# Two tiles to a burst in the first pair's attention, and raw x laid out tile by tile

## The chip, the cores and the metric

The kernel runs on one core of a Trainium2 chip. The metric is the device time of one execution in microseconds (us); lower is better. TensorE (PE) multiplies matrices and writes to PSUM, a memory of eight banks; VectorE (DVE) and ScalarE (ACT) read PSUM and do the elementwise work; GpSimd (POOL) does elementwise work in SBUF; SyncE (SP) issues the DMAs.

## The reference

Attention over chunks of 64 tokens, and a mixture of four experts on its output, whose every expert sees every token:

```
scores = scale * matmul(q_c, k_c.T)          # per head and chunk of 64 tokens, 8 heads of 64
attn   = softmax(scores)
out    = matmul(attn, v_c)                   # -> x, 4608 tokens x 512
p      = domain_probs / sum(domain_probs)
for e in range(4):
    h = max(x @ w1[e], 0)                    # 512 -> 1024
    y += p[:, e] * (h @ w2[e])               # 1024 -> 512
```

All data are fp32. The products of the experts are made of three matmuls each, from a high and a low part of both factors.

## The kernel before

The 4608 tokens are nine sub-blocks of 512 (four tiles of 128 tokens each). The first sub-block goes through the experts alone, in eight plain passes (expert by half of the hidden units, n = 0 to 7). The other eight are four pairs; each pair goes through eight later passes, in which seven products of half-size blocks take the place of eight. While one pair is in the experts, the attention of the next pair is worked in between, so that TensorE always has the experts' matmuls to go on with. The attention of pair 0 lies beside the first sub-block's plain passes 1 to 6, that of pair 1 beside the later passes of pair 0, and so on.

A plain pass has eight steps of TensorE: four hidden blocks (`plain_hidden`, 12 matmuls of 128x128 by 512 columns, then a relu on ScalarE and its low part on VectorE) and four output tiles (`Tile.whole`, 12 matmuls, added into `acc` on VectorE). `issue` calls `beside.go()` before each step; `go` runs the generator `attention` up to its next `yield`. What is put into `deferred` there is written out after the step's own instructions. Each engine runs its instructions in the order in which the program writes them.

One tile of attention is 16 score matmuls of 64x64 (32 rows in the trace), a softmax (maximum, subtraction, exponential, sums, reciprocal, scaling), a transpose within blocks on VectorE, a placing copy on ScalarE (`a_place`) and 16 value matmuls. In pair 0 a tile takes five steps: `a_less_max` and `a_exps`, then `a_weights` and `a_transpose`, then `a_place`, then two steps of room. After them `a_next` writes a *burst*: the values of this tile and the scores of the next, 32 matmuls. There are nine such bursts in pair 0: scores alone, seven of both kinds, values alone. Scores stand in one half of `psa` (two PSUM banks of their own) and the values, as well as the softmax sums, in the other half. The tile's q and k come into `qk_in`, its v into `v_in`.

Pairs 2 and 3 already work two tiles to a burst (`attend_two`, `two_next`): the scores of both tiles fill both halves of `psa`, the values go into the banks B1 and C1, the sums into B1, and q, k and v of the odd tile are loaded into parts of `xraw` that are not yet filled with x. Pair 1 works tile by tile, and keeps its x in memory (`x_kept`) until `x_back` loads it.

The other six PSUM banks (A0, A1, B0, B1, C0, C1) are handed out in turn by `bank()` when no name is given: in plain passes every hidden block and output tile takes the next one, so that a bank comes round after six. The last plain pass and the later passes name theirs.

`xraw` holds the 1024 tokens of a pair as `[P, NK, PAIR * SUB]`: for each partition four rows of 1024 tokens; a tile is 128 columns of each row. The class `Tokens` makes from it the sums and the high and low parts that the later passes multiply.

Of the kernel before, what the change touches and what calls it, by code (L numbers as in the profile page):

```python
# [15 lines left out]
P = 128  # L16
# [15 lines left out]
def chunk_attention_moe(ctx: ExitStack, tc: tile.TileContext, qk, v, v0, dp, w1, w2, out):  # L32
# [180 lines left out]
    def a_copy(t):  # L213
        pair, i = divmod(t - NT, PAIR * NT)
        if pair == 1:
            tile_x = scratch[0][:, :SUB].rearrange("p (j q) -> p j q", j=NK)
        else:
            tile_x = of_tiles(pair, i, 1)
        to = tile_x.rearrange("p j (c q) -> p c j q", c=2)
        av = blocks(1)  # L220
        nc.scalar.copy(out=to[:, :, 0::2], in_=av[:, :, 0::2])
        nc.scalar.copy(out=to[:, :, 1::2], in_=av[:, ::-1, 1::2])
        if pair == 1:
            nc.sync.dma_start(out=x_kept[:, :, i * P : (i + 1) * P], in_=tile_x)

    def of_tiles(pair, i, n):
        if pair not in xraw:
            xraw[pair] = xpool.tile([P, NK, PAIR * SUB], F32, name="xraw")  # L230
        return xraw[pair][:, :, i * P : (i + n) * P]

    def two_load(t, i):
        if i == 0:
            a_load(t)
            return
        pair = (t - NT) // (PAIR * NT)
        to = of_tiles(pair, 6, 2).rearrange("p (g x) (h s) -> p g x h s", x=2, h=HG)
        st[t] = {"x": to}
        for g in range(2):  # L240
            nc.sync.dma_start(out=to[:, g], in_=qk[t, g].rearrange("c d x h s -> (c d) x h s"))

    def two_load_v(t, i, odd):
        if i and not odd:
            pair, j = divmod(t - NT, PAIR * NT)
            st[t]["v"] = of_tiles(pair, 7 if j == 7 else 5, 1).rearrange("p j (h d) -> p j h d", h=2)
        elif not odd:
            st[t]["v"] = load.tile([P, NK, 2, C], F32, name="v_in")
        to = st[t]["v"].rearrange("p (g i) h d -> p g i h d", i=2)
        of = v[t - NT].rearrange("p (g i h) d -> p g i h d", g=2, i=2)  # L250
        if not odd:
            nc.sync.dma_start(out=to[:, :, 0], in_=of[:, :, 0])
            return
        for half in range(2):
            rows, other = slice(half * C, (half + 1) * C), slice((1 - half) * C, (2 - half) * C)
            nc.sync.dma_start(out=to[rows, :, 1], in_=of[other, :, 1])
# [5 lines left out]
            q, k = (s["x"][of_half(c), head // HG, x, head % HG] for x in range(2))  # L262
            nc.tensor.matmul(s["sc"][of_half(half), c, slot], lhsT=q, rhs=k, start=True, stop=True)  # L263

    def two_sums(t):
        z = bank("B1")[:, : 2 * HG].rearrange("p (c j) -> p c j", c=2)
        st[t]["r"] = inverse_sums(st[t]["sc"], z)

    def two_weights(t):
        two_sums(t)  # L270
        a_scale(t)
        a_transpose(t)

    def two_next(t, scores):

        av = None
        if t is not None:
            av = [bank(name).rearrange("p (i j k) -> p i j k", i=2, k=C) for name in ("B1", "C1")]
            for i in range(2):
                s = st.pop(t + i)  # L280
                for c, half, slot, head in quarters():
                    nc.tensor.matmul(  # L282
                        av[half][of_half(slot % 2), i, head // 2],
                        lhsT=s["v"][of_half(half), head // 2, head % 2],
                        rhs=s["pt"][of_half(half), c, slot], start=True, stop=True,
                    )
        if scores is not None:
            for i in range(2):
                two_scores(scores + i, i)
        if av:  # L290
            pair, j = divmod(t - NT, PAIR * NT)
            to = of_tiles(pair, j, 2).rearrange("p j (i c q) -> p i j c q", i=2, c=2)
# [4 lines left out]
    x_kept = dram.tile([P, NK, PAIR * SUB], F32, name="x_kept")  # L297

    def x_back():
        xraw[1] = xpool.tile([P, NK, PAIR * SUB], F32, name="xraw")  # L300
        for k in range(NK):
            nc.sync.dma_start(out=xraw[1][:, k], in_=x_kept[:, k])


    def less_max(a):
# [15 lines left out]
    def scale(e, a, r):  # L321
        nc.vector.tensor_tensor(out=e, in0=a, in1=r, op=ALU.mult)

    def attention(pair, close):

        first = (1 + pair * PAIR) * NT
        last = first + PAIR * NT  # L330
        a_load(first)
        yield
        a_next(None, first)
        for t in range(first, last):

            if close:
                steps = (a_less_max, a_exps), (a_weights, a_transpose), (None, a_place), (None, None)
            else:
                steps = (a_less_max, a_exps), (a_sums, a_scale), (a_transpose, None), (a_place, None)
            for now, then in steps:  # L340
# [8 lines left out]
    def a_next(t, after, loads=True):  # L349
# [8 lines left out]
        if loads and after is not None:  # L358
            a_load_v(after)
            a_load_after(after)  # L360

# [69 lines left out]
    def hi_part(src, t):  # L431
        nc.scalar.copy(out=t[0], in_=src)
# [218 lines left out]
    class Tokens:  # L651
# [4 lines left out]
        def __init__(self, pair):  # L656
            x = xraw.pop(pair)
            for k in range(2):
                for s in range(2):
                    rows, toks = slice(2 * k, 2 * k + 2), slice(s * SUB, (s + 1) * SUB)  # L660
                    setattr(self, f"b{k + 1}{s + 1}", x[:, rows, toks])

        def less(self, name, a, b, out, eng=None):
            (eng or nc.vector).tensor_tensor(
# [2 lines left out]
            setattr(self, name, out)  # L667

        def sum1(self):
            self.less("t1", "b12", "b11", load.tile([P, 2, SUB], F32, name="qk_in"))  # L670

        def sum2(self):
            self.less("t2", "b22", "t1", self.b22)

        def sum2_apart(self, eng):

            self.t2 = [att.tile([P, SUB], F32, name=name) for name in ("e", "pt")]
# [3 lines left out]
        def sum4_apart(self):  # L681

            for k, t in enumerate(self.t2):
                nc.vector.tensor_tensor(out=psa[:, k], in0=self.b21[:, k], in1=t, op=ALU.subtract)
            self.t4 = psa

        def split2(self):
            i = self.KEYS["t2"]
            x_alloc(i)
            for k, t in enumerate(self.t2):  # L690
                hi_part(t, [part[:, k] for part in xt[i]])

        def lo2(self, k):
            lo_part(nc.vector, self.t2[k], [part[:, k] for part in xt[self.KEYS["t2"]]])

        def sum3(self, eng=None):
            self.less("t3", "b22", "b12", self.b12, eng)
# [4 lines left out]
        def hi(self, name):  # L702
            i = self.KEYS[name]
            x_alloc(i)
            hi_part(getattr(self, name), xt[i])

        def lo(self, name, eng=None):
            lo_part(eng or nc.vector, getattr(self, name), xt[self.KEYS[name]])


    TERMS = ((0, 0), (0, 1), (1, 0))
# [568 lines left out]
    class Beside:  # L1280


        def __init__(self, pair, close):
            self.steps = attention(pair, close)

        def go(self):
            next(self.steps, None)
# [188 lines left out]
    def attend(at, pair, places, i):  # L1476
        t = (1 + pair * PAIR) * NT + i
        after = t + 1 if i + 1 < PAIR * NT else None
        if i == 0:
            add(at, 13, lambda: a_next(None, t, False))  # L1480
# [4 lines left out]
        add(at, places[2], lambda: a_next(t, after, False))  # L1485
        if after:
            add(at, places[2] + 1, lambda: a_softmax(after))
            loads(at, places[2], after)
# [261 lines left out]
        by_halves(steps["b"])  # L1750

    with tc.manual_schedule():
        beside = Beside(0, True)
# [53 lines left out]
```

## Time and profile before

| | |
|---|---|
| median of 3 runs | 1480.26 us (1477.7 to 1481.23) |
| the profiled execution | 1478.61 us, span 1476.7 us |
| TensorE busy | 1461.3 us, 99% of the span |
| VectorE, GpSimd, ScalarE busy | 1094.4, 976.5, 623.3 us |
| TensorE's granted clock | full in all 40 slices |
| share of TensorE in the chain that ended last | 93% |

The span is from the first to the last instruction of the profiled execution. Busy time counts a matmul until its modelled end, so it overlaps with the next one; whether TensorE loses time is therefore read from the starts of its matmuls and from its waits.

### The profile page before, as it was taken

The page shows a single profiled execution, that of the slowest core. Times are in us where ns is not written, and L with a number is a line of the kernel's source. Part 1 is how long each engine was busy: PE and PEld are TensorE (multiplying, and loading weights), DVE is VectorE, ACT ScalarE, POOL GpSimd, SP SyncE. Part 2 cuts the span into 40 slices and gives each one's busy share as a digit, 9 for nine tenths or more (in the row PEclk, how much of TensorE's full clock was granted, in tenths as well). Part 3 has the DMA queues.
Part 4 walks back from the last instruction along what each step waited for, and adds up shares of the span by engine and source line. Part 5 has one row for each costly group of instructions (what it writes and reads, how often), then busy time and mean ns, then how long its engine had stood idle before and what let it go on. Part 6 is the DMA issues. An engine that isn't in the chain of part 4 may idle for free.

```text
span 1476.7 us, 23341 instructions
## 1 busy us (share of the span) xinstructions
PE 1461.3 (99%) x8556; PEld 1199.8 (81%) x8556; DVE 1094.4 (74%) x1492; ACT 623.3 (42%) x1165; POOL 976.5 (66%) x728
## 2 busy tenths in 40 slices
PE   8999999999999999999999999999999999999998
PEld 7888887887878878888888888888888888888887
DVE  5566658899898886787767977777668866666665
ACT  4556635545454534434433434444334333233332
POOL 5778887888877884555557656555557655555555
PEclk9999999999999999999999999999999999999999
DMA  9798886878777789766565688676565695565655
GB/s 308 266 342 313 302 316 209 272 240 266 237 252 240 241 260 259 241 219 230 194 210 198 219 231 279 218 241 198 195 203 197 201 255 198 198 207 194 207 190 151
DMA packets 201250, 346.94 MB, mean 235 GB/s; under 512 B 70176, under 2 KB 114480, under 8 KB 200752
## 3 DMA queue, kind: packets, MB, share of 16 engines
q1 hardware_dynamic: 201136, 345.45, 71.6%
q8 instruction: 68, 1.11, 0.3%
q14 instruction: 46, 0.38, 0.1%
HBM read 274.01 MB, written 71.38 MB: 234 GB/s over the span
## 4 chain that ended last, share of the span: by engine, by line
PE 93%; DVE 3%; DMA 2%; POOL 1%; issue 1%; ACT 0%; SPq 0%; DVEq 0%; POOLq 0%; ACTq 0%
PE A L717 48%; PE C L717 27%; PE B L717 14%; DMA v_in<-in_v 1%; DVE xraw L560 1%; DMA wf<-in_w 1%; PE psa L208 1%; PE psa L263 1%; PE B L282 0%; PE psa L161 0%; DMA wf<-w 0%; DVE acc L942 0%; POOL hf L435 0%; POOL hf L895 0%; POOL wf L573 0%
## 5 line engine op out<-in xcount | busy, mean ns | idle before, releaser
L895 POOL TENSOR_TENSOR hf<-wraw,hf 128x512 fp32r<-128x512 f32 x384 | 508.0, 1341 | 227.6 <-ACT hf L892 226.1
L717 PE MATMUL A<-hf,wf 128*128 128x512 f32 x1536 | 391.9, 391 | 1.8 <-DVE acc L942 1.8
L717 PE MATMUL A<-xh,wf 128*128 128x512 f32 (+1 forms) x1104 | 380.6, 388 | 1.2 <-POOL wf L573 1.2
L892 ACT CAST hf<-wraw 128x512 fp32r<-128x512 f32 x384 | 233.9, 622 | 295.6 <-DVE wraw L886 98.4
L717 PEld LDWEIGHTS A<-hf,wf 128*128 128x128 f32 x1536 | 286.2, 188 | 64.7 <-DVE acc L942 4.3
L717 PEld LDWEIGHTS A<-xh,wf 128*128 128x128 f32 x1104 | 206.7, 188 | 44.3 <-POOL wf L573 1.6
L780 ACT COPY s<-A 128x512 f32<-128x512 f32 x192 | 112.8, 587 | 291.1 <-PE A L717 290.8
L717 PE MATMUL A<-xl,wf 128*128 128x512 f32 (+1 forms) x552 | 213.8, 388 | 0.2 <-DVE xl L435 0.2
L942 DVE TENSOR_TENSOR acc<-A,acc 128x512 f32<-128x512 f32 x232 | 157.9, 681 | 65.0 <-PE A L717 64.6
L717 PE MATMUL C<-xh,wf 128*128 128x512 f32 (+1 forms) x600 | 203.6, 386 | 2.3 <-DMA wf<-w 1.5
L717 PE MATMUL C<-hf,wf 128*128 128x512 f32 x768 | 195.1, 389 | 0.2
L717 PEld LDWEIGHTS C<-hf,wf 128*128 128x128 f32 x768 | 143.9, 188 | 31.1 <-DVE acc L942 1.0
L717 PEld LDWEIGHTS C<-xh,wf 128*128 128x128 f32 x600 | 111.4, 188 | 25.9 <-DVE acc L942 1.9
L886 POOL TENSOR_TENSOR wf<-wraw,wf 128x512 f32<-128x512 f32 x31 | 40.1, 1293 | 136.2 <-DVE wf L880 134.5
L717 PE MATMUL B<-xh,wf 128*128 128x512 f32 (+1 forms) x376 | 125.2, 384 | 1.0 <-POOL wf L573 1.0
L895 POOL TENSOR_TENSOR hf<-wf,hf 128x512 fp32r<-128x512 f32 x64 | 91.1, 1424 | 48.6 <-ACT hf L892 48.6
L717 PEld LDWEIGHTS A<-xl,wf 128*128 128x128 f32 x552 | 103.5, 188 | 21.9 <-DVE xl L435 0.7
L717 PE MATMUL C<-xl,wf 128*128 128x512 f32 (+1 forms) x300 | 114.6, 385 | 0.2 <-DVE xl L435 0.2
L942 DVE TENSOR_TENSOR acc<-C,acc 128x512 f32<-128x512 f32 x120 | 82.6, 689 | 43.2 <-PE C L717 40.6
L886 DVE TENSOR_TENSOR wraw<-wf,wraw 128x512 f32<-128x512 f32 x64 | 97.5, 1523 | 5.2 <-POOL hf L895 4.1
L717 PE MATMUL B<-hf,wf 128*128 128x512 f32 x384 | 97.9, 390 | 0.0
L886 POOL TENSOR_TENSOR wraw<-wraw 128x512 f32<-128x512 f32 x63 | 92.2, 1464 | 0.0
(218 smaller groups left out, 1983.2 us busy)
## 6 DMA issues: line engine op xcount, KB each, us to landing
wf<-w SPq DMA_DIRECT2D x399, 512.0 KB, 4.3
w<-wf SPq DMA_DIRECT2D x49, 512.0 KB, 5.2
w<-hf SPq DMA_DIRECT2D x28, 512.0 KB, 7.2
qk_in<-in_qk SPq DMA_DIRECT2D x24, 512.0 KB, 5.4
w<-hf SPq DMA_DIRECT2D x42, 256.0 KB, 4.7
wf<-in_w SPq DMA_DIRECT2D x19, 512.0 KB, 7.2
ws<-p_t SPq DMA_DIRECT2D x24, 256.0 KB, 4.1
xraw<-in_w SPq DMA_DIRECT2D x24, 256.0 KB, 4.8
```

What stands on the lines that cost most here:

```text
L208: nc.tensor.matmul(av[of_half(slot % 2), half, head // 2], lhsT=s["v"][of_half(half), head], rhs=s["pt"][of_half(half), c, slot], start=Tr ...
L263: nc.tensor.matmul(s["sc"][of_half(half), c, slot], lhsT=q, rhs=k, start=True, stop=True)
L560: (eng or nc.vector).tensor_tensor(out=to, in0=a, in1=b, op=op)
L717: nc.tensor.matmul(out, lhsT=lhs(k, a), rhs=rhs(k, b), start=first and i == 0, stop=last and i == len(parts) - 1, skip_group_check=not (fi ...
L780: nc.scalar.copy(out=t, in_=self.a)
L886: (eng or nc.vector).tensor_tensor(out=self.values[place, k], in0=self.values[a, k], in1=self.values[b, k], op=op)
L892: nc.scalar.copy(out=self.part(name, 0)[:, k], in_=self.values[name, k])
L895: (eng or nc.gpsimd).tensor_tensor(out=self.part(name, 1)[:, k], in0=self.values[name, k], in1=self.part(name, 0)[:, k].bitcast(F32), op=A ...
L942: nc.vector.tensor_tensor(out=acc[key], in0=src, in1=acc[key], op=ALU.add)
```

## The change

Pair 0 now works like pairs 2 and 3: `attention` loads two tiles ahead (`two_load`, `two_load_v`), and `two_next` writes one burst for two tiles. The ten steps of two tiles are the same as before in number and content: maximum, sums, place and two steps of room for the even tile, then for the odd tile. The bursts in pair 0 are five: scores of two tiles, three times values and scores of two tiles, values of two tiles. The values and the sums take banks in turn (`bank(None)`): two for each burst and one for each tile's sums, 16 in all. The transpose on VectorE and the placing copy stay where they were. q and k of the odd tile go into tiles 6 and 7 of `xraw`, v into tile 5 (of the last odd tile, into tile 7).

`xraw` is laid out `[P, PAIR * NT, NK, P]`: for each partition the eight tiles one behind another, each 2 KB in one piece. All that reads or writes it follows: a tile's store to `x_kept` is 2 KB a partition in place of four pieces of 512 bytes, the load of the odd tile's q and k is one DMA in place of two, and the operations of `Tokens` read eight runs of 128 in place of two of 512.

```diff
     def of_tiles(pair, i, n):
-        if pair not in xraw:
-            xraw[pair] = xpool.tile([P, NK, PAIR * SUB], F32, name="xraw")
-        return xraw[pair][:, :, i * P : (i + n) * P]
+        return (xraw[pair] if pair in xraw else x_tiles(pair))[:, i : i + n]
...
-        to = of_tiles(pair, 6, 2).rearrange("p (g x) (h s) -> p g x h s", x=2, h=HG)
+        to = of_tiles(pair, 6, 2).rearrange("p g (x i) (j s) -> p g x (i j) s", x=2, s=C)
         st[t] = {"x": to}
-        for g in range(2):
-            nc.sync.dma_start(out=to[:, g], in_=qk[t, g].rearrange("c d x h s -> (c d) x h s"))
+        nc.sync.dma_start(out=to, in_=qk[t].rearrange("g c d x h s -> (c d) g x h s"))
...
-    def two_sums(t):
-        z = bank("B1")[:, : 2 * HG].rearrange("p (c j) -> p c j", c=2)
+    def two_sums(t, name=None):
+        z = bank(name)[:, : 2 * HG].rearrange("p (c j) -> p c j", c=2)
...
-    def two_next(t, scores):
+    def two_next(t, scores, banks=("B1", "C1")):
...
-            av = [bank(name).rearrange("p (i j k) -> p i j k", i=2, k=C) for name in ("B1", "C1")]
+            av = [bank(name).rearrange("p (i j k) -> p i j k", i=2, k=C) for name in banks]
...
-    def attention(pair, close):
+    def attention(pair):
...
+        def loads(t, i):
+            for odd in (False, True):
+                two_load_v(t, i, odd)
+            if t + 2 < last:
+                two_load(t + 2, i)
+
+        for i in range(2):
+            two_load(first + i, i)
         yield
-        a_next(None, first)
-        for t in range(first, last):
...
+        two_next(None, first)
+        for t in range(first, last, 2):
+            loads(t, 0)
+            for i in range(2):
+                u = t + i
                 yield
-                if now:
-                    now(t)
-                if then:
-                    deferred.append(lambda then=then: then(t))
-            yield
-            a_next(t, t + 1 if t + 1 < last else None)
+                a_less_max(u)
+                deferred.append(lambda u=u: a_exps(u))
+                yield
+                two_sums(u)
+                a_scale(u)
+                deferred.append(lambda u=u: a_transpose(u))
+                yield
+                deferred.append(lambda u=u, i=i: a_place(u, ("pt", "e")[i]))
+                yield
+                yield
+                if i == 0:
+                    loads(t + 1, 1)
+            two_next(t, t + 2 if t + 2 < last else None, (None, None))
```

On TensorE, the burst after the third tile of pair 0 (pass 2, between its second and third output tile), before:

```order
217 L717 MATMUL A_1192<-hf_1030,hf_1009 128x512 x6
218 L717 MATMUL A_1192<-hf_1098,hf_1114 128x512 x6
219 L103 MATMUL B_1206<-ident,s_1103 128x128
220 L103 MATMUL B_1211<-ident,s_1103 16x128
221 L208 MATMUL psa<-pt,v_in 64x64 x16
222 L161 MATMUL psa<-qk_in 64x64 x16
223 L717 MATMUL C_1265<-hf_1030,hf_1009 128x512 x6
224 L717 MATMUL C_1265<-hf_1098,hf_1114 128x512 x6
```

The same place after the change (an even tile's end, so no burst is due; the two transposes of the probabilities stand alone):

```order
248 L729 MATMUL A_1212<-hf_1013,hf_992 128x512 x6
249 L729 MATMUL A_1212<-hf_1117,hf_1133 128x512 x6
250 L103 MATMUL A_1226<-ident,s_1122 128x128
251 L103 MATMUL B_1231<-ident,s_1122 16x128
252 L729 MATMUL B_1249<-hf_1013,hf_992 128x512 x6
253 L729 MATMUL B_1249<-hf_1117,hf_1133 128x512 x6
```

The burst's 32 matmuls have gone to the burst of the odd tile before and to that after, and the output tiles behind it stand in other banks.

On VectorE, the softmax of pair 0's first tile, in pass 1, before:

```order
48 L725 SCALAR_TENSOR_TENSOR hf_757<-A_758,hf_757 128x512
49 L315 TENSOR_REDUCE psa<-psa 128x8
50 L316 TENSOR_SCALAR psa<-psa 128x8
51 L318 RECIPROCAL z_785<-psa 128x8
52 L322 TENSOR_TENSOR e<-psa,z_785 128x512
53 L725 SCALAR_TENSOR_TENSOR hf_757<-A_789,hf_757 128x512
54 L188 STREAM_TRANSPOSE psa<-e 128x2x256
```

and after the change:

```order
48 L737 SCALAR_TENSOR_TENSOR hf_775<-A_776,hf_775 128x512
49 L316 TENSOR_REDUCE A_801<-psa 128x8
50 L317 TENSOR_SCALAR A_801<-A_801 128x8
51 L319 RECIPROCAL z_804<-A_801 128x8
52 L323 TENSOR_TENSOR e<-psa,z_804 128x512
53 L737 SCALAR_TENSOR_TENSOR hf_775<-B_808,hf_775 128x512
54 L188 STREAM_TRANSPOSE psa<-e 128x2x256
```

The order is the same; the sums stand in a bank of the rotation (A), and the next hidden block has moved on to bank B.

On the DMA queue of SyncE, the rows around the end of tile 0 in pass 1, before:

```order
35 L424 DMA hf_812<-in_w 128x2048
36 L535 DMA w_1_2_106<-hf_699 128x1024
37 L535 DMA w_1_5_109<-hf_699 128x1024
38 L131 DMA v_in<-in_v 128x2x128
39 L135 DMA v_in<-in_v 64x2x128 x2
40 L121 DMA qk_in<-in_qk 128x2x512
```

and after:

```order
36 L431 DMA hf_831<-in_w 128x2048
37 L542 DMA w_1_2_106<-hf_701 128x1024
38 L542 DMA w_1_5_109<-hf_701 128x1024
39 L253 DMA xraw<-in_v 128x2x128
40 L257 DMA xraw<-in_v 64x2x128 x2
41 L242 DMA xraw<-in_qk 128x2x512
```

The loads at the end of an even tile stand where they stood, but go into parts of `xraw` that were last read by the burst before; the one load that has moved is that of the second tile's q and k, which is now issued in the startup, right behind the first tile's.

## Rows read from the trace of the kernel before

**Rows 1.** The page, busy us, share of the span and instructions by engine.

```profile
PE 1461.3 (99%) x8556; PEld 1199.8 (81%) x8556; DVE 1094.4 (74%) x1492; ACT 623.3 (42%) x1165; POOL 976.5 (66%) x728
```

**Rows 2.** Waits of TensorE, whole span: us in total, times, longest.

```profile
PE C L717 <- DMA wf<-w: 1.5, 1, 1.5
...
PE A L717 <- POOL wf L573: 1.2, 1, 1.2
PE B L717 <- POOL wf L573: 1.0, 1, 1.0
```

**Rows 3.** Windows: stretch, us, busy by engine, granted clock, DMA share, GB/s.

```profile
20.00:25.00 5.00, 4.83 (x36) 4.12 (x34) 4.55 (x11) 4.84 (x11) 4.94 (x4) 1.00 0.65 232
33.00:200.00 167.00, 166.84 (x1215) 136.55 (x1215) 106.08 (x147) 97.47 (x195) 136.85 (x101) 1.00 0.84 297
600.00:1440.00 840.00, 840.00 (x4584) 694.05 (x4583) 610.69 (x837) 318.00 (x584) 493.55 (x371) 1.00 0.66 212
```

**Rows 4.** Chain that ended last: start, us, what; 24 matmuls in a row.

```profile
62.23 5.44 PE A L717 x24
```

**Rows 5.** Timeline of TensorE, pair 0: start us, us, line, tile, count.

```profile
37.86 2.91 PE L717 MATMUL C<-hf,hf 128*128 128x512 f32 x12
...
41.37 3.03 PE L717 MATMUL A<-hf,hf 128*128 128x512 f32 x12
...
70.00 0.39 PE L717 MATMUL B<-xh,wf 128*128 128x512 f32 x1
70.32 0.69 PE L208 MATMUL psa<-pt,v_in 64*64 64x64 f32 x32
...
71.47 0.50 PE L717 MATMUL B<-xh,wf 128*128 128x512 f32 x1
71.80 0.39 PE L717 MATMUL B<-xl,wf 128*128 128x512 f32 x1
...
157.96 2.88 PE L717 MATMUL C<-hf,hf 128*128 128x512 f32 x12
...
161.40 3.02 PE L717 MATMUL C<-hf,hf 128*128 128x512 f32 x12
...
175.13 5.96 PE L717 MATMUL C<-hf,hf 128*128 128x512 f32 x24
```

**Rows 6.** Timeline of TensorE around two-tile bursts of pairs 2 and 3.

```profile
571.06 0.39 PE L717 MATMUL C<-xh,wf 128*128 128x512 f32 x1
...
572.52 1.66 PE L717 MATMUL A<-hf,wf 128*128 128x512 f32 x6
...
610.88 0.39 PE L717 MATMUL C<-xh,wf 128*128 128x512 f32 x1
...
613.28 1.65 PE L717 MATMUL A<-hf,wf 128*128 128x512 f32 x6
...
1046.95 0.39 PE L717 MATMUL C<-xh,wf 128*128 128x512 f32 x1
...
1048.36 1.66 PE L717 MATMUL A<-hf,wf 128*128 128x512 f32 x6
```

**Rows 7.** Softmax sums on VectorE (line 315): ns min/median/max, first and last start.

```profile
L315 DVE TENSOR_REDUCE psa<-psa x17: 689/690/700, 20.5 to 444.5; 128x8 f32<-128x512 f32 x17
L315 DVE TENSOR_REDUCE B<-psa x16: 689/690/690, 578.4 to 1038.7; 128x8 f32<-128x512 f32 x16
```

**Rows 8.** Copies of two tiles' values on ScalarE (line 295), as rows 7.

```profile
L295 ACT COPY xraw<-B x16: 372/376/379, 612.4 to 1048.7; 128x256 f32<-128x256 f32 x16
```

**Rows 9.** Timeline: last matmul of a hidden block, and the last reader of its bank.

```profile
145.34 0.39 PE L717 MATMUL C<-xh,wf 128*128 128x512 f32 x1
...
148.51 0.69 DVE L725 SCALAR_TENSOR_TENSOR hf<-C,hf 128x512 fp32r<-128x512 f32 x1 [4.14 <-ACT hf L724]
```

**Rows 10.** Waits of SyncE's DMA queue from 30 to 200 us.

```profile
SPq L131 <- PE psa L161: 16.2, 4, 8.5
```

**Rows 11.** The stores to x_kept (line 224): ns min/median/max, first and last start.

```profile
L224 SPq DMA_DIRECT2D x_kept<-xraw x8: 567/574/590, 266.9 to 453.2; - x8
```

More of the change, by code (lines that the diff above doesn't have):

```diff
@@ L217, in a_copy @@
         else:
-            tile_x = of_tiles(pair, i, 1)
+            tile_x = of_tiles(pair, i, 1)[:, 0]
         to = tile_x.rearrange("p j (c q) -> p c j q", c=2)
@@ L223, in a_copy, with x_tiles @@
         if pair == 1:
-            nc.sync.dma_start(out=x_kept[:, :, i * P : (i + 1) * P], in_=tile_x)
+            nc.sync.dma_start(out=x_kept[:, i], in_=tile_x)
+    def x_tiles(pair):
+        xraw[pair] = xpool.tile([P, PAIR * NT, NK, P], F32, name="xraw")
+        return xraw[pair]
     def of_tiles(pair, i, n):
-        if pair not in xraw:
-            xraw[pair] = xpool.tile([P, NK, PAIR * SUB], F32, name="xraw")
-        return xraw[pair][:, :, i * P : (i + n) * P]
+        return (xraw[pair] if pair in xraw else x_tiles(pair))[:, i : i + n]
     def two_load(t, i):
@@ L245, in two_load_v @@
             pair, j = divmod(t - NT, PAIR * NT)
-            st[t]["v"] = of_tiles(pair, 7 if j == 7 else 5, 1).rearrange("p j (h d) -> p j h d", h=2)
+            st[t]["v"] = of_tiles(pair, 7 if j == 7 else 5, 1)[:, 0].rearrange("p j (h d) -> p j h d", h=2)
         elif not odd:
@@ L291, in two_next @@
             pair, j = divmod(t - NT, PAIR * NT)
-            to = of_tiles(pair, j, 2).rearrange("p j (i c q) -> p i j c q", i=2, c=2)
+            to = of_tiles(pair, j, 2).rearrange("p i j (c q) -> p i j c q", c=2)
             for half in range(2):
@@ L295, in two_next @@
                     nc.scalar.copy(out=to[:, :, odd::2, half ^ odd], in_=av[half][:, :, odd::2])
-    x_kept = dram.tile([P, NK, PAIR * SUB], F32, name="x_kept")
+    x_kept = dram.tile([P, PAIR * NT, NK, P], F32, name="x_kept")
     def x_back():
-        xraw[1] = xpool.tile([P, NK, PAIR * SUB], F32, name="xraw")
-        for k in range(NK):
-            nc.sync.dma_start(out=xraw[1][:, k], in_=x_kept[:, k])
+        x = x_tiles(1)
+        for i in range(0, PAIR * NT, 2):
+            nc.sync.dma_start(out=x[:, i : i + 2], in_=x_kept[:, i : i + 2])
     def less_max(a):
@@ L322, in scale, with a_next @@
         nc.vector.tensor_tensor(out=e, in0=a, in1=r, op=ALU.mult)
-    def attention(pair, close):
+    def attention(pair):
         first = (1 + pair * PAIR) * NT
         last = first + PAIR * NT
-        a_load(first)
-        yield
-        a_next(None, first)
-        for t in range(first, last):
[L336 to L340, printed above, removed]
-                yield
-                if now:
-                    now(t)
-                if then:
-                    deferred.append(lambda then=then: then(t))
-            yield
-            a_next(t, t + 1 if t + 1 < last else None)
-    def a_next(t, after, loads=True):
+        def loads(t, i):
[5 more added lines that the diff above has]
+            two_load(first + i, i)
+        yield
+        two_next(None, first)
[3 more added lines that the diff above has]
+                u = t + i
+                yield
+                a_less_max(u)
[11 more added lines that the diff above has]
+            two_next(t, t + 2 if t + 2 < last else None, (None, None))
+    def a_next(t, after):
         if t is not None:
@@ L357, in a_next @@
             a_copy(t)
-        if loads and after is not None:
-            a_load_v(after)
-            a_load_after(after)
     KEYS = {"a11": 0, "a12": 1, "a22": 2, "s1": 3, "s2": 4, "s3": 5, "s4": 6}
@@ L669, in sum1 @@
         def sum1(self):
-            self.less("t1", "b12", "b11", load.tile([P, 2, SUB], F32, name="qk_in"))
+            self.less("t1", "b12", "b11", self.by_tile(load.tile([P, 2, SUB], F32, name="qk_in")))
         def sum2(self):
@@ L675, in sum2_apart @@
         def sum2_apart(self, eng):
-            self.t2 = [att.tile([P, SUB], F32, name=name) for name in ("e", "pt")]
+            self.t2 = [att.tile([P, NT, P], F32, name=name) for name in ("e", "pt")]
             for k, t in enumerate(self.t2):
@@ L690, in split2 @@
             for k, t in enumerate(self.t2):
-                hi_part(t, [part[:, k] for part in xt[i]])
+                hi_part(t, [self.by_tile(part)[:, k] for part in xt[i]])
         def lo2(self, k):
-            lo_part(nc.vector, self.t2[k], [part[:, k] for part in xt[self.KEYS["t2"]]])
+            lo_part(nc.vector, self.t2[k], [self.by_tile(part)[:, k] for part in xt[self.KEYS["t2"]]])
         def sum3(self, eng=None):
@@ L704, in hi @@
             x_alloc(i)
-            hi_part(getattr(self, name), xt[i])
+            hi_part(getattr(self, name), [self.by_tile(part) for part in xt[i]])
         def lo(self, name, eng=None):
-            lo_part(eng or nc.vector, getattr(self, name), xt[self.KEYS[name]])
+            parts = [self.by_tile(part) for part in xt[self.KEYS[name]]]
+            lo_part(eng or nc.vector, getattr(self, name), parts)
     TERMS = ((0, 0), (0, 1), (1, 0))
@@ L1280, in chunk_attention_moe, with __init__ @@
     class Beside:
-        def __init__(self, pair, close):
-            self.steps = attention(pair, close)
+        def __init__(self, pair):
+            self.steps = attention(pair)
         def go(self):
@@ L1479, in attend @@
         if i == 0:
-            add(at, 13, lambda: a_next(None, t, False))
+            add(at, 13, lambda: a_next(None, t))
             add(at, 14, lambda: a_softmax(t))
@@ L1484, in attend @@
         add(at, places[1], lambda: a_place(t))
-        add(at, places[2], lambda: a_next(t, after, False))
+        add(at, places[2], lambda: a_next(t, after))
         if after:
@@ L1752, in chunk_attention_moe @@
     with tc.manual_schedule():
-        beside = Beside(0, True)
+        beside = Beside(0)
         startup(beside)
```

13 lines of the change are left out of this document (8 added, 5 removed).

## The prediction

> **What bounds the kernel now.** I read the page first: TensorE is busy for 1461.3 of 1476.7 us [rows 1], so time can only be won or lost where TensorE does something else than the experts' matmuls, or waits. Next come its waits: the largest three after the startup are 1.5 us for a load and 1.2 and 1.0 us for GpSimd [rows 2]. All of these lie after pair 0's attention. The windows say the same by stretch: in the one that holds pair 0's attention, 33 to 200 us, TensorE is idle for 0.16 us, and from 600 to 1440 us, where pairs 2 and 3 are worked, for nothing at all [rows 3]. The granted clock is full in each. So VectorE, ScalarE, GpSimd and the DMA queue have slack wherever the change touches them, and the change has to be priced on TensorE: by the time that its attention bursts take from the experts' matmuls.
>
> That price is read from starts, because busy times overlap. 24 matmuls in a row take 5.44 us, 0.227 us each [rows 4]. A burst costs what lies between the time when the next big matmul would have started and the time when it did, and its exit, the extra time of the first matmul behind it.
>
> **The change, part by part.**
>
> *The bursts.* Of the old ones, the first (scores alone) lies between 12 matmuls from 37.86 us, which end their turn at 40.58, and the next at 41.37: 0.79 us. One with values and scores: 70.00 plus 0.23 to 71.47, 1.24 us; this is the cheapest of the seven, and I take it for all. Values alone: 157.96 plus 2.72 to 161.40, 0.72 us [rows 5]. Sum 0.79 + 7 x 1.24 + 0.72 = 10.19 us. The exits: 71.47 to 71.80 in place of 0.23 is 0.10 us, and the twelve matmuls behind the other two show 3.03 and 3.02 in place of 2.88, so 0.15 and 0.14 [rows 5]; 0.13 each, nine times.
>
> The new bursts stand in the trace already, in pairs 2 and 3 [rows 6]: scores of two tiles 571.29 to 572.52, 1.23 us; values and scores of two tiles 611.11 to 613.28, 2.17 us; values of two tiles 1047.18 to 1048.36, 1.18 us. In pair 0 there will be one, three and one: 1.23 + 3 x 2.17 + 1.18 = 8.92 us. So the bodies save 1.27 us and four exits less save 0.52: **1.8 us**. It is the same number of small matmuls; what goes is four entries and four exits.
>
> The Trainium skill (TensorEngine Tiling (Array Packing), Key Properties) says that a change of tiling mode, not of tile, drains the engine. By that alone the four bursts that vanish would be worth their entries and exits, some 0.9 us by the gaps of 0.09 and 0.13 us on the two sides of a burst in the trace. The rows say twice that, since a merged burst also pays the fill at its start and end just once.
>
> *Bounds of this term.* If the merged bursts in pair 0 cost what two single ones do, nothing is saved: 0. If each of the four paid back a whole values-only burst with its exit, 4 x 0.85 = 3.4 us. The rows of pairs 2 and 3 are the same instructions on the same shapes, so I keep 1.8.
>
> *The two transposes of the probabilities* in pass 2 stood beside an old burst and shared its entry. They now stand alone. Between nothing and a whole exit and entry, 0.25 us; I take **0.15 us lost**.
>
> *The softmax sums* in a bank of the rotation: the reduction takes 690 ns into `psa` and 690 ns into a bank [rows 7]. Nothing by itself; what it does to the banks is a rival below.
>
> *The placing copies, the exponentials, the copies of the values* are as many and as large as before; the copies, 376 ns each [rows 8], come four at a time every ten steps instead of two every five. What hides them is the step of TensorE that runs beside them, 2.7 us: nothing. If that cover goes, a relu queued behind an odd burst's copies comes 0.75 us later than now, and the hidden block's bank with it (below).
>
> *The loads.* The same bytes; one load of 512 KB, q and k of the second tile, moves into the startup, where SyncE reaches it near 20 us. From 20 to 25 us the DMA engines are 65% busy [rows 3]. Nothing waits for the store of factors queued behind it in the next microseconds; first use at 40.6 us. Nothing. At the end of even tiles, SyncE no longer waits for a burst before it can reload: of 16.2 us in four such waits [rows 10] about half go. TensorE was not waiting for what stood behind them, so nothing again, at most what the rivals say.
>
> *Where the gain may be taken back.* In pass 6 the first two output tiles start at 175.13 us and show 5.96 us where 24 matmuls and their tail take 5.60: 0.36 us lost, on w2's low parts from GpSimd [rows 5]. All but the last burst's saving, some 1.6 us, is made before that point. If GpSimd comes no sooner, all of it turns into a longer wait there; if it follows TensorE, through ScalarE's relus of the hidden blocks, nothing does. Its last 5 us of work start behind casts that ScalarE queues after such a relu, which speaks for the second; I take **0.3 us lost** of 0 to 1.6.
>
> *The layout.* The `Tokens` operations read eight runs of 128 in place of two of 512. No row of before has just this pattern. Below nothing too: a shorter run has no way to speed an engine that goes element by element. Above: a tenth more on a dozen operations of 1 to 2 us for each pair, 2 us of VectorE and GpSimd, in stretches where TensorE has no wait for them [rows 3]: nothing on TensorE. The stores to `x_kept` cost SyncE 574 ns to issue now [rows 11], in four pieces a partition; in one piece less, over eight stores 1 or 2 us of SyncE, which TensorE does not wait for at those places. The load of the odd tile's q and k in pairs 2 and 3, one issue for two, likewise: TensorE has no wait there at all.
>
> Sum: -1.8 + 0.15 + 0.3 = -1.35 us. Against the profiled execution's own 1478.61 us (span 1476.7) that is 1477.3; against the median of the runs, which is 1.65 us above the profiled execution, **1478.9 us**. A difference of 0.3%, 4.4 us, is about what a measurement of this kernel tells from no change.
>
> **The rivals.**
>
> *All of it is taken back.* The wait in pass 6 grows by what was won before it, and the waits of 1.2 and 1.0 us on GpSimd in the ring of pass 9 [rows 2] by the rest. For it: GpSimd is busy for 137 of 167 us in that stretch [rows 3]. Against: its idle times there end with ScalarE and TensorE. Time: 1480.3 us, no change. 0.12.
>
> *Slower: the banks run short.* This is the one on the other side. With 16 more turns in pair 0's 40 steps, a bank comes round after as little as three steps, where it was six; counted through, two whole steps lie between a block's end and the next writer at the tightest place inside pair 0, 2 x 2.72 = 5.4 us, often with a burst of 2.2 us more. In pass 7 the named bank B1 comes one step after the last hidden block, 2.7 us. Today's slowest reader: a hidden block ends at 145.57 us, and the low part of its relu at 149.20, 3.6 us later, since ScalarE had casts queued before the relu [rows 9]. The rival decides if this delay passes 5.4 us, so if ScalarE falls back by 1.8 us more. Seven tight places that each overrun by 1 us or so make 7 us: 1480.3 + 7 - 1.3 = 1486 us. Against it: the copies of an odd burst are only two more than now, 0.75 us, and the copies of the even bursts are gone. 0.06.
> The Trainium skill (TensorEngine Tiling (Array Packing), PSUM Bottleneck) warns of just that: packing speeds TensorE and not the emptying of PSUM. Here the emptying has its slack, by the rows, of 1.8 us.
>
> *Faster: SyncE's freed waits bring weights earlier.* About 8 us of waits of the DMA queue vanish in passes 1 and 4, and one-piece stores free more in pair 1. If that removed all three waits of rows 2 (3.7 us) besides, the time would be 1480.26 - 1.35 - 3.7 = 1475.2 us, faster by 0.34%. Against: those waits lie 40 us and more behind pair 0's last load. 0.04.
>
> **How the numbers follow.** The forecast, only the bursts' overhead is saved, has 0.76; the 0.02 left is for a layout that costs more than thought (some 1485 us). The time is the forecast's, 1478.9 us. The range must hold the first rival (1480.3), the bounds of the burst term (0 to 3.4 us: 1480.7 to 1477.3) and the spread of the runs, 1.8 us either way round their middle: 1474.5 to 1482.5. Faster by over 0.3%: 0.05, the faster rival and a little of the forecast's edge. Slower: 0.08, the banks and the layout. The same: 0.87.
>
> **What would show each step right or wrong.** In the timeline of pair 0, five bursts: bodies near 1.2, 2.2 and 1.2 us, and no 64x64 matmuls at the ends of even tiles. TensorE's later steps 1.3 us sooner from about 200 us on, if nothing is taken back; the two output tiles in pass 6 would show a row beyond 5.96 us if it is. In the waits, no new line of TensorE for a relu, an `acc` or a sum in passes 1 to 7; such lines of 1 us would be the banks. SyncE's waits for a burst about half. The `Tokens` operations on GpSimd within a tenth of what they took. The prediction is wrong if the time leaves 1474.5 to 1482.5 us; it is right for the wrong reason if the bursts do not shrink, or if the gain is made in another stretch than 40 to 200 us.

## The result, and the profile after

The median of 22 runs of the changed kernel is 1481.80 us (1478.87 to 1486.35), that of 22 runs of the kernel before beside them 1478.49 us. The ratio is 1.0020, with a 95% interval of 1.0014 to 1.0027: 3.3 us slower, where 1.35 us were to be gained. It is within the 0.3% that the prediction called no change, and within its range, but on the other side: the interval leaves no change out.

The profiled execution took 1483.95 us, its span is 1482.1 us. The waits of TensorE, in total, times, and the longest; they answer to [rows 2]:

```profile
engine line waited for: us in total, times, longest us
PE A L729 <- DVE acc L954: 3.1, 3, 1.3
PE B L1110 <- DVE e L323: 2.1, 2, 1.9
PE C L729 <- issue: 1.8, 1, 1.8
PE C L729 <- DMA wf<-w: 1.6, 1, 1.6
PE A L729 <- issue: 1.6, 1, 1.6
PE C L729 <- POOL hf L442: 1.3, 1, 1.3
...
PE A L729 <- POOL wf L580: 1.2, 1, 1.2
PE B L729 <- POOL wf L580: 1.0, 1, 1.0
```

Three lines are new: two waits for "issue", which is time in which TensorE waited for nothing that the profile shows, and one for a low part from GpSimd (L442). The line for `acc` has one wait more, of 1.25 us near 494 us (see the last section). The waits for a load and for GpSimd's parts in the ring stand as they were.

The timeline of TensorE at the three new places (start, duration, and in brackets the idle time ahead), to be held against [rows 5]:

```profile
100.76 0.39 PE L729 MATMUL B<-xh,wf 128*128 128x512 f32 x1
101.08 0.27 PE L283 MATMUL B<-pt,v_in 64*64 64x64 f32 x1
...
102.70 0.53 PE L264 MATMUL psa<-xraw 64*64 64x64 f32 x22
105.00 0.40 PE L729 MATMUL C<-xh,wf 128*128 128x512 f32 x1 [1.78 <-issue]
...
134.38 1.65 PE L729 MATMUL A<-hf,hf 128*128 128x512 f32 x6
137.60 1.52 PE L729 MATMUL A<-hf,hf 128*128 128x512 f32 x6 [1.57 <-issue]
...
155.28 2.12 PE L729 MATMUL C<-hf,hf 128*128 128x512 f32 x7
158.69 4.15 PE L729 MATMUL C<-hf,hf 128*128 128x512 f32 x17 [1.29 <-POOL hf L442]
```

The first is right behind the second burst of values and scores; the second is six matmuls behind the third such burst, in the middle of an output tile; the third is in pass 5. From starts: six matmuls from 134.38 are done issuing at 135.74, so 1.86 us are lost before 137.60; seven from 155.28 end at 156.87, so 1.82 us before 158.69. The three lose 5.5 us.

The windows by stretch answer to [rows 3] (busy time and count on TensorE, its weight loads, VectorE, ScalarE, GpSimd; then granted clock, DMA share, GB/s):

```profile
10.00:12.00 2.00, 2.00 (x56) 2.00 (x56) 0.93 (x2) 1.06 (x2) 0.86 (x1) 0.72 1.08 377
12.00:14.00 2.00, 1.32 (x17) 1.13 (x14) 1.10 (x3) 1.25 (x3) 0.40 (x1) 0.50 1.06 392
...
16.00:18.00 2.00, 2.00 (x12) 2.00 (x12) 0.00 (x0) 0.00 (x0) 0.00 (x0) 0.57 1.02 410
...
33.00:200.00 167.00, 162.22 (x1206) 133.99 (x1205) 102.96 (x145) 93.52 (x191) 133.54 (x99) 1.00 0.82 285
```

TensorE is busy for 162.2 of 167 us in pair 0's stretch, where it was 166.84. Besides, this one execution had half the clock (0.50, the lower level of 1.2 GHz) for some 7 us of the startup, and lost 2 us there against the second profile below, which is free of it. Of 33 executions of the changed kernel nine have a mean clock of 0.998 or less, of 98 of the kernel before six; whether the change has a part in it is open.

What the two waits for "issue" stand beside is in the DMA view. Queue 8 loads instructions: packets, MB, share. The first row is of the whole span, the others are of the stretches 102.6 to 102.8 and 135.0 to 135.1 us:

```profile
q8 instruction: 68, 1.11, 0.3%
...
q8 instruction: 1, 0.02, 29.4%
...
q8 instruction: 1, 0.02, 66.8%
```

68 packets of 16 KB for 8556 matmuls and as many weight loads (the page's counts): 252 of these instructions to a packet, and some waits on semaphores between them. So TensorE's program comes in blocks, and at both places a block begins to load only 0.5 to 0.7 us before TensorE runs dry. It takes 0.94 us (29.4% of 16 engines' 0.2 us) and 1.07 us.

### The profile page after: what moved, and what is told of

Same layout as the page of the kernel before. It is cut to its first block, busy times and chain, and to the rows that moved or that the text cites. A ratio compares the mean times of both kernels' runs of the same rounds, so it can differ in the third digit from the quotient of the medians.

```text
span 1482.1 us, 23338 instructions
## 1 busy us (share of the span) xinstructions
PE 1461.7 (99%) x8556; PEld 1201.7 (81%) x8556; DVE 1091.8 (74%) x1492; ACT 622.6 (42%) x1165; POOL 976.1 (66%) x728
## 4 chain that ended last, share of the span: by engine, by line
PE 91%; DVE 3%; POOL 2%; DMA 2%; issue 1%; ACT 0%; SPq 0%; POOLq 0%; DVEq 0%; ACTq 0%
PE A L729 47%; PE C L729 27%; PE B L729 15%; POOL hf L442 1%; DMA xraw<-x_kept 1%; PE psa L264 1%; DVE xraw L567 1%; PE B L283 1%; DMA wf<-w 0%; DVE acc L954 0%; POOL hf L907 0%; POOL wf L442 0%; DMA w<-hf 0%; POOL wf L580 0%; PE psa L208 0%
## 5 line engine op out<-in xcount | busy, mean ns | idle before, releaser
L729 PE MATMUL A<-xh,wf 128*128 128x512 f32 (+1 forms) x1128 | 388.8, 388 | 1.2 <-POOL wf L580 1.2
L729 PEld LDWEIGHTS A<-xh,wf 128*128 128x128 f32 x1128 | 211.5, 188 | 45.3 <-POOL wf L580 1.6
L729 PE MATMUL A<-xl,wf 128*128 128x512 f32 (+1 forms) x564 | 218.6, 388 | 0.3 <-DVE xl L442 0.3
L729 PE MATMUL B<-xh,wf 128*128 128x512 f32 (+1 forms) x352 | 117.4, 383 | 1.0 <-POOL wf L580 1.0
```

The source lines that it names most:

```text
L729: nc.tensor.matmul(out, lhsT=lhs(k, a), rhs=rhs(k, b), start=first and i == 0, stop=last and i == len(parts) - 1, skip_group_check=not (fi ...
```

## The experiments

**Theory 1, the instructions come late.** A burst of two tiles is 128 small matmuls and 128 weight loads, done in 2.17 us: about as many instructions as a block has. If a block ends on the burst's first instructions, the burst uses up the whole next one before the one after it has come. **Theory 2, the banks**, is the slower rival of the prediction: a bank, or a relu behind the copies of the burst, comes late. The place of an instruction in the stream matters to the first alone.

**The changed kernel again**, for a second profile.

> The changed kernel, unchanged, for a second profile. Theory 1: the two waits of 1.8 us are at the same two places, behind the bursts near 101 and 132 us (some 2 us sooner if the clock stays full at the start), each with a block's load of TensorE's instructions that begins during or after the burst; median 1480.5 to 1482 us. If the waits were chance: elsewhere or absent in this profile.

1481.60 us, ratio 1.0022 (1.0013 to 1.0031). Its profile has the full clock at the start, and was of one of its shorter executions (1479.68 us). Both waits are there, at the same instructions, and shorter:

```profile
102.43 0.39 PE L729 MATMUL C<-xh,wf 128*128 128x512 f32 x1 [1.10 <-DVE hf L737]
...
134.17 1.09 PE L729 MATMUL A<-hf,hf 128*128 128x512 f32 x4 [0.71 <-issue]
```

The first is now put down to VectorE's low part of a relu, which in the other profile was done 1.4 us before the matmul (at 103.6 us), and in this one 0.7 us before it: such a releaser is inferred, and here it is not the cause. Queue 8 began to load a block between 100.0 and 100.2 us, within the burst, and between 131.7 and 131.9 us, as the next burst ended. So place and cause repeat, and the size varies from one execution to the next: 1.8 and 1.9 us, or 1.1 and 1.0.

**The layout alone**, with the old attention of pair 0, and **the kernel before again**.

```diff
-            xraw[pair] = xpool.tile([P, NK, PAIR * SUB], F32, name="xraw")
...
+        xraw[pair] = xpool.tile([P, PAIR * NT, NK, P], F32, name="xraw")
```

> The kernel before with the tile-by-tile layout of raw x alone; the attention of pair 0 as before, one tile to a burst. If the loss lies in the bursts of pair 0 and what follows from them: as before, ratio 0.9993 to 1.0007, and no wait of TensorE that the kernel before does not show. If the layout is the cause (longer sums and parts on VectorE and GpSimd): the new waits after 200 us, such as 1.4 us for an acc at 494 us, appear here too, ratio 1.001 to 1.003.

> The kernel before, unchanged, for its granted clock in many runs. If the half clock near 11 to 17 us belongs to the change: all runs at 1.000, ratio 1.000 within 0.0007. If it comes by chance in both kernels: some runs at 0.997 to 0.999, as the changed kernel shows, each about 2 us longer per 0.0015 of mean clock, ratio 1.000 all the same.

All that reads or writes raw x follows, as in the change. 1478.74 us, ratio 1.0002 (0.9994 to 1.0011), and 1478.26 us, 0.9999 (0.9990 to 1.0008). The layout costs and brings nothing that can be measured; no line of "issue" stands in its waits. The loss comes with pair 0's bursts. None of these eleven executions of the kernel before has the low mean clock, but six of its 87 others do, so it comes with both kernels.

**The same program 32 and 96 instructions further on.** Each warming matmul at the start is written as two of half the columns, or as four.

```diff
-        for _ in range(n):
-            nc.tensor.matmul(idle, lhsT=zeros[:, :P], rhs=zeros, start=True, stop=True)
+        for i in range(2 * n):
+            cols = slice(i % 2 * (SUB // 2), (i % 2 + 1) * (SUB // 2))
+            nc.tensor.matmul(idle[:, cols], lhsT=zeros[:, :P], rhs=zeros[:, cols], start=True, stop=True)
```

> The changed kernel with each warming matmul at the start written as two of half the columns: 16 matmuls more (32 instructions with their weight loads), as many columns as before, nothing else. Every later instruction of TensorE stands 32 places further on in its stream. Theory 1 (instructions come late): TensorE's instructions are loaded in blocks of 256, and a burst of two tiles is 256 instructions in 2.2 us; where the end of a block falls on a burst's start, the next block comes after the burst has run out. Then the waits of 1.8 us that end at 105.0 and 137.6 us are both gone, 3.6 us in all, and the median falls from 1481.8 to between 1478.2 and 1479.5 us (ratio 0.9998 to 1.0007), since GpSimd's wait at 158.7 us may take some back. Theory 2 (banks or the copies of the burst): places in the instruction stream don't matter, both waits stay, median 1481.8 us, ratio 1.002.

> The same with four matmuls of a quarter of the columns for each warming matmul: 96 instructions more. Theory 1: the ends of the blocks now fall some 48 matmuls of 512 columns before the bursts of pair 0; both 1.8 us waits are gone here too, 1478.2 to 1479.5 us. By the same count one block's end comes close to a burst of pairs 2 and 3 (near 698 and 931 us); if TensorE has nothing to wait for ahead of those bursts, its fetch runs ahead and no wait appears. Theory 2: both waits stay, 1481.8 us.

1477.14 and 1477.19 us, both 0.9993 (0.9984 to 1.0002), so 4.5 us less than the changed kernel, a larger gain than was expected. The waits of the first, with no line of "issue" left, and its timeline at the second burst:

```profile
PE A L729 <- DVE acc L954: 1.8, 2, 0.9
PE C L729 <- POOL hf L442: 1.3, 1, 1.3
...
98.65 0.39 PE L729 MATMUL B<-xh,wf 128*128 128x512 f32 x1
...
101.05 0.50 PE L729 MATMUL C<-xh,wf 128*128 128x512 f32 x1
```

98.65 plus 0.23 to 101.05 is the burst of 2.17 us, and nothing behind it. The block that was late now begins to load between 91 and 92 us. Banks, relus and copies are as before, so theory 2 falls.

With 96 instructions more a block ends, by a count of the trace, some eight matmuls into a burst of pair 2, which begins at 690.96 us. As the expectation said, nothing is lost there (the burst takes its 2.17 us): the next block begins to load at once, between 691.2 and 691.3 us, and is needed only at 694.8. The row of queue 8 in that stretch:

```profile
q8 instruction: 1, 0.02, 58.6%
```

So the end of a block in a burst does not make a wait by itself; the load has to begin late as well.

**Eight instructions further on.** Only four warming matmuls are halved.

> The changed kernel with only four of the ten warming matmuls ahead of the first transposes written as two halves: 4 matmuls, 8 instructions more. In the changed kernel the two late blocks end on the first instructions of a burst; here they end some 4 matmuls of 512 columns ahead of it, and the 256 instructions that follow are still nearly all the burst's, done in 2.6 us. Theory 1a (what counts is that the block's end lies ahead of the burst's first matmul, so that the next block is asked for before the burst): no wait of 1.8 us, 1477.1 us as with 32 instructions, ratio 0.9985 to 1.0002. Theory 1b (what counts is how long the 256 instructions last): a block's load took 3.9 us from the burst's start to the next matmul at 105.0, so with 2.6 us some 1.3 us are left of each of the two waits, and the median is near 1479.7 us.

1480.71 us, 1.0015 (1.0006 to 1.0024): between the two. The profile shows why. Behind the second burst there is no wait, although its block of 256 instructions still passes in 2.6 us: the load began between 94.2 and 94.4 us, 4.7 us ahead of the burst. That is theory 1a: the next block begins to load well ahead of what TensorE executes, where the end of the old block lies ahead of the burst's first matmul. The changed kernel's own first long burst, at 71.31 us, agrees: a block began to load at 68.7 us, and nothing was lost. Why the load begins late where the block ends inside a burst of pair 0, and not in pair 2, was not tried.

Behind the third burst the wait is there:

```profile
130.73 0.72 PE L729 MATMUL A<-hf,hf 128*128 128x512 f32 x2
133.41 1.31 PE L729 MATMUL A<-hf,hf 128*128 128x512 f32 x5 [1.96 <-issue]
```

Here the load began at 131.0 us, 0.3 us behind the burst, which began at 128.65. The wait stands two large matmuls behind the burst, where it stood six behind it: four matmuls with their weight loads are the eight instructions, so the wait kept its place in the stream while the program moved on. Eight instructions were too few to bring this block's end out of the burst: the expectation took both ends to lie equally deep, and they don't.

**Controls.** The kernel before with its warming halved, and both kernels with the warming as it was and 16 matmuls of 8 columns behind it, in the time when TensorE waits for the first softmax:

```diff
         keep_warm(WAITS["softmax"])
+        for _ in range(16):
+            nc.tensor.matmul(idle[:, :8], lhsT=zeros[:, :P], rhs=zeros[:, :8], start=True, stop=True)
```

> The kernel before with its warming matmuls halved as in the run with 32 instructions more: a control. A single-tile burst is 128 instructions, so no block of 256 can be used up within a burst, wherever it ends. Theory 1: nothing changes, 1478.2 to 1479 us, ratio 0.9994 to 1.0006. If the finer warming itself (the clock at the start, or some other order there) gained the 4.7 us: near 1474 us, ratio 0.997.

> The changed kernel with its warming matmuls as they were, and 16 matmuls of 8 columns behind them, in the time in which TensorE waits for the first softmax: the stream is shifted by the same 32 instructions, the warming is not made finer. Theory 1: both waits behind the bursts of pair 0 (1.1 and 1.0 us in the second profile of the changed kernel, 1.8 and 1.9 in the first) are gone, the median falls by 2 to 3.6 us to between 1478 and 1479.5 us, ratio 0.9995 to 1.0007, if the 1.4 us that the control gained came from the finer warming; to 1477.1 us, ratio 0.999, if they came from the shift itself. Theory 2 (banks): 1481.6 us, ratio 1.002.

> The kernel before with the same 16 matmuls of 8 columns: the control for that run. If the finer warming gave the 1.4 us: 1478.5 us, ratio 0.9993 to 1.0007. If the places of the blocks' ends matter for the kernel before too: 1477.3 us, ratio 0.999.

The kernel before: 1477.29 us (0.9990, 0.9981 to 0.9999) and 1477.47 us (0.9993, 0.9984 to 1.0002). The changed kernel: 1477.53 us (0.9992, 0.9983 to 1.0001). So the shift itself gains 1.3 us in the kernel before too, which theory 1 did not foresee and finer warming does not explain: that control's expectation failed. Two thirds of it are found, at the very end. SyncE's queue there, first of the kernel before in its second profile, then with the 16 small matmuls:

```profile
1471.01 2.44 SPq L1707 DMA_DIRECT2D out<-s  x3
```

```profile
1470.58 2.05 SPq L1709 DMA_DIRECT2D out<-s  x3
```

From the last matmul's start to the span's end the two profiles of the kernel before and that of the layout alone take 4.9 to 5.1 us, all nine others 4.1 to 4.2 us: 0.8 us. In the three, the last block of TensorE's instructions begins to load 4.2 to 4.4 us before the last matmul, in the others 9.7 to 14.5 us before it. Whether that load slows the stores was not tried, and 0.5 us of the control's gain is found nowhere. The changed kernel, without any shift, already has the short end.

With both streams moved by the same 32 instructions, then, the changed kernel (1477.53) is where the kernel before is (1477.47): what the bursts save is taken back, which leaves the third wait.

**The third wait.** In pass 5 GpSimd makes the low parts of w2 one after the other. In the kernel with 32 instructions more it stood idle for 1.54 us before 145.12, for a cast that ScalarE had queued behind a placing copy. In this run the casts of step 0 of pass 5 stand ahead of the copy.

```diff
-    def issue(steps, at, beside, ahead=False):
+    def issue(steps, at, beside, ahead=False, early=()):
...
             step()
+            if i in early:
+                late = at.pop(i) + late
             for f in late:
                 f()
...
-            issue(steps, at, beside, True)
+            issue(steps, at, beside, True, (0,) if n == 5 else ())
```

> The kernel with 32 instructions more (1477.14 us), and in step 0 of pass 5 ScalarE's four casts of w2's parts written ahead of the placing copies instead of behind them. The theory of the third wait: TensorE waits 1.8 us near 153 us, since GpSimd makes the low parts of w2's last quarter too late; GpSimd stood idle 1.54 us before 145.12, waiting for a cast that ScalarE had queued behind the placing copies; the two bursts that no longer stand between pass 4's end and this place had hidden that. Then the wait falls to about 0.3 us and the median to between 1475.6 and 1476.6 us, ratio 0.998 to 0.999. Rival: another wait takes its place (GpSimd's next parts, or the placing copies at the next burst), and the median stays at 1477.1 us.

1475.42 us, ratio 0.9980 (0.9971 to 0.9989): faster than both kernels, and just below what was expected. ScalarE, and TensorE where the wait had been:

```profile
142.50 1.13 ACT L439 CAST hf<-acc 128x512 fp32r<-128x512 f32 x2
143.53 1.14 ACT L439 CAST hf<-wf 128x512 fp32r<-128x512 f32 x2
144.57 0.58 ACT L194 COPY pt<-psa 128x512 f32<-128x512 f32 x1
...
149.97 4.27 PE L729 MATMUL C<-hf,hf 128*128 128x512 f32 x18
```

The 18 matmuls go through without a stop. The row of one matmul that waits for GpSimd in pass 9 in every kernel, the first of the two in [rows 2], serves as a milestone. Before (first profile), the changed kernel (both), 16 small matmuls, casts first:

```profile
241.88 0.74 PE L717 MATMUL A<-xh,wf 128*128 128x512 f32 x2 [1.19 <-POOL wf L573]
```

```profile
247.07 0.73 PE L729 MATMUL A<-xh,wf 128*128 128x512 f32 x2 [1.18 <-POOL wf L580]
```

```profile
243.71 0.73 PE L729 MATMUL A<-xh,wf 128*128 128x512 f32 x2 [1.18 <-POOL wf L580]
```

```profile
241.78 0.74 PE L729 MATMUL A<-xh,wf 128*128 128x512 f32 x2 [1.18 <-POOL wf L580]
```

```profile
239.81 0.73 PE L729 MATMUL A<-xh,wf 128*128 128x512 f32 x2 [1.17 <-POOL wf L580]
```

From the kernel before to the last, the matmul comes 2.07 us sooner with the waits gone: that is what the bursts save. The wait itself stays at 1.2 us, so GpSimd follows TensorE here. Not all of it reaches the end: in the last kernel's profile an `acc` takes 1.25 us of it near 490 us (last section).

## Why the prediction was wrong

That the time lies within the stated range is luck. The range was laid around a median of three runs, 1480.26 us, and 22 runs of the same kernel gave 1478.49; laid around that it ends at 1480.7, below the 1481.8 that were measured. (Its lower end is 1 us below what its terms give, 1477.3 less 1.8.) What made the kernel slower is in none of its terms.

**The bursts: right, and the saving a little larger.** In the last kernel, where nothing blurs them, the first burst lies between 12 matmuls from 37.98 and the next at 41.96 us: 1.26 us (predicted 1.23). The three of values and scores take 2.17 us each (2.17), the last 1.18 (1.18): 8.95 us against 8.92. The exits are 0.11 us (0.13 was taken). The milestone's 2.07 us are more than the sum without the term for GpSimd (1.65 us), mainly since the cheapest old burst, 1.24 us, was taken for all seven. The others take 1.28 to 1.35, as this one, 54.89 plus 0.23 to 56.46:

```profile
54.89 0.39 PE L717 MATMUL B<-xh,wf 128*128 128x512 f32 x1
...
56.46 0.50 PE L717 MATMUL C<-hf,hf 128*128 128x512 f32 x1
```

The old burst with the two transposes took 1.46 us, 0.1 to 0.2 more than the rest. Alone they cost 0.23, so at most 0.1 us was lost by them, not 0.15.

**The step that failed** stands in the prediction as "The rows of pairs 2 and 3 are the same instructions on the same shapes, so I keep 1.8." The rows give the burst's own length, and that carried over. They don't tell what it takes to bring 256 instructions in time for 2.2 us: that the instructions are there was put at nothing, without a row for it, and in pairs 2 and 3 no wait behind a burst showed it. The waits behind two of the three long bursts cost 3.6 us in one profile and 2.1 in the other; the medians of the changed kernel and of the one with 16 small matmuls differ by 4.1 us, in which the half clock of some executions has a share. A single-tile burst is 128 instructions, and the rest of its block takes 64 matmuls of 0.227 us, 14.5 us, so by this count pair 0 could not run dry in the kernel before, and its trace could not show the wait there. The row of queue 8 stands on that kernel's page, with the same 68 packets.

The Trainium skill (Runtime: NRT & Kernel Launch, Instruction fetch mechanics) says that an engine's program is refilled in blocks of 16 KiB, 256 instructions, while it executes the block before, and that crossing from one to the next is mostly hidden. The trace agrees on the size (68 packets for 17,112 matmuls and weight loads). On "hidden" the measurement decides: here 1.0 to 1.9 us show behind two bursts of the changed kernel, and 2.2 us behind one with eight instructions more.

**What GpSimd takes back: mis-sized, and in another pass.** Of 0 to 1.6 us, 0.3 was taken, in pass 6. Pass 6 takes nothing: its row of 5.96 us [rows 5] is 5.97 in the last kernel, which comes there 2.06 us sooner. The loss is 1.82 us, in pass 5, and there the kernel before had no slack. Its low part of w2 was done at 153.92 us, and the 24 matmuls of which the eighth needs it passed in 5.70 us, where 24 without a wait take 5.60. First the kernel before, then pass 6 in the last kernel:

```profile
151.36 2.56 POOL L435 TENSOR_TENSOR hf<-ws,hf 128x512 fp32r<-128x512 f32 x2
...
152.43 5.70 PE L717 MATMUL B<-hf,hf 128*128 128x512 f32 x24
```

```profile
173.07 5.97 PE L729 MATMUL B<-hf,hf 128*128 128x512 f32 x24
```

With 32 instructions more TensorE begins these 24 matmuls 2.67 us sooner, at 149.76 us, and the low part is done only 0.8 us sooner, at 153.12. The reason for the low value ("it follows TensorE, through ScalarE's relus") holds for ScalarE's relus but not for the placing copies of 2.1 us, which stand between a relu and GpSimd's casts and whose time does not shrink with the bursts. The first rival, all taken back, was nearly right for this part in the amount, though not in the place.

**The banks: right to give them little.** With 32 instructions more, passes 1 to 7 show no wait of TensorE for a relu, an `acc` or a sum, in spite of the rotation's 16 added turns.

**Startup, layout, loads, copies: right at nothing.** The layout alone is within 0.1% of the kernel before; the moved load shows in no wait of TensorE. SyncE's waits for TensorE between 30 and 200 us fall from 25.9 to 10.2 us, by over half as predicted, and TensorE gets nothing from it.

**The sum.** 1478.5 us before; -2.1 for the bursts, +1.8 for GpSimd, -0.8 for the last stores make 1477.4 us, which is the kernel with 16 small matmuls (1477.53). It closes no better than the 0.5 us of the control's gain that are found nowhere. The two late blocks, 2.1 to 3.6 us by the profiles, bring it to between 1479.5 and 1481.0. The executions of the changed kernel with a mean clock of 0.999 or more have a median of 1480.9, all of them 1481.8.

## What to carry to other kernels

Count instructions, not only time: a burst of small matmuls that holds as many instructions as one block, in less time than a block takes to come, can stall the engine behind it, and whether it does depends on how many instructions stand anywhere before it. Where the waits show "issue" behind a burst, look for a packet of the instruction queue in that stretch, and move the stream by a few dozen instructions in idle time before changing the algorithm. When an engine on the path gets faster by removing filler, follow the next engine's queue to its next deadline through everything that stands between, copies included.

## What was not expected of the hardware

TensorE's instructions come in packets of 16 KB, each of which took about 1 us. Where the load began only within a burst or right behind it, the matmul that was held up started 2.3 to 2.6 us after the load began (102.7 to 105.0, 135.0 to 137.6); where the block's end lay four large matmuls ahead of the burst, the load began 4.7 us ahead of it and nothing was lost.

Moving the same instructions by 32 places gained 1.3 us in the kernel before, of which 0.8 us lie at the last stores. In three of the twelve profiles, all three with the new bursts, one with no shift and two with, an `acc` of VectorE makes TensorE wait 1.25 us near 490 us. Four other profiles with the new bursts don't have it, and what decides it stays open.
